# Reordering score tiles, reduction units, reciprocals and loads in the attention stage of a pooled-attention and two-MoE kernel

## The chip, the cores and the metric

The kernel runs on one core of a Trainium2 chip. The metric is device time in microseconds (us) of one execution. A core has five engines with instruction queues of their own: PE (TensorE, matmuls; its weight loads are listed as PEld), DVE (VectorE), ACT (ScalarE), POOL (GpSimd) and SP (SyncE, which here only issues transfers). Each queue runs strictly in its written order and waits on semaphores.

## The reference

```python
q_pool = q.reshape(B, H, S // factor, factor, D).mean(axis=3)       # B 4, H 8, S 1152, D 64, factor 2
scores = scale * np.matmul(q_pool, k.transpose(0, 1, 3, 2))
scores = scores - np.max(scores, axis=-1, keepdims=True)
attn = np.exp(scores)
attn = attn / (np.sum(attn, axis=-1, keepdims=True) + 1e-09)
x = np.matmul(attn, v)                    # then laid out as 2304 tokens x 512
h = x @ w_in;  x = (h - np.tanh(h)) @ w_out                         # 512 -> 2048 -> 512
h = x @ w_in2; x = (h * (1.0 / (1.0 + np.exp(-1.702 * h)))) @ w_out2
```

## The kernel before, in words

The attention stage comes first and takes about a third of the time; two MLP layers follow and are not touched here. The order of all instructions is written out by hand: what the code says first stands first in an engine's queue.

Attention works on 16 pairs of heads (`p`), each head on 64 of the 128 partitions, and each pair has two halves (`x` = 0 and 1, 288 pooled queries each). So there are 32 halves, `h = 2p + x`; "even" means x = 0. In a half, PE computes nine score tiles (S, `scores`, L429), each of four pairs of matmuls: keys' high part times queries' high part, keys' low part (`kl`), queries' low part (`ql`), and a selector matrix times `row`, which subtracts the row's maximum. ACT turns each tile into probabilities (`pf`, L435). Then PE multiplies them with v (`products`, L480) and sums them with ones (L493), and ACT copies the result out (`u`, L501).

The maxima for the next pair come from eleven units (`unit`): matmuls into an `mx` tile, which DVE reduces into a column of `mt` (L371). Units 0 to 8 of pair p+1 run within the halves of pair p; they are X (512 wide; unit 6 in four narrow pieces). Units 9 and 10 of a pair, called C, run in its own even half. The strings in `usual` say in which order tiles and units stand on PE: the first string for even halves, the second for odd ones. After unit 6 and after unit 10, `max_rows` and `send_rows` reduce `mt`, transpose it to `tt`, and send it by six (part 0) or four (part 1) small transfers on SP into `row` and `cr`. Part 0 is needed by the fourth step of the first score tile of the next pair's even half, part 1 by its odd half.

All tiles of PSUM (`sc`, `mx`, `acc`) come in rotation from four buffers, so a tile waits until the one four places earlier in PE's order has been read.

Sums of the probabilities are shared: POOL adds tiles into `sum` (L446), DVE adds the last four into `rest` (L464). The sums are gathered by four small transfers into `s9` (`sums`), `recip` takes the reciprocals on DVE (L522, L523) and writes them to `rd` in DRAM, `spread` reads `rd` back to all partitions (`rbd`, which waits for `rd` to land), and `normalise` multiplies (L540).

Jobs are hung on places of a half by `at(h, place, job)` and run in this order: "first", "start", tiles and units, "load", "pre", "gp", the products, "end", "pool". Loads of later pairs: keys `kr` (L290, 576 KB), `v` (576 KB) and pooled queries `qs` (288 KB) on SP; two transfers on POOL's queue add into DRAM (`qd`, L281 and L338). `prep_kl` on POOL waits for the last DVE job noted in `last["v"]`. MLP weights are prepared meanwhile: one weight takes four halves, one DVE step (L143, L149, L156 or L163) at "end" of each; the first step also takes magnitudes on ACT (`wa`, L142), at "end" of halves 2, 6, 10, ..., 26.

```python
at(h, "start", sums, p - 1)
at(h, "pre" if h == NH - 2 else "end", recip, p - 1)
at(h + 1, "start", spread, p - 1)
at(h + 1, "end", normalise, p - 1)
at(h - 4, "load", load_sum, p)
at(h - 4, "first", load_k, p)
```

Of the kernel before, what the change touches and what calls it, by code (L numbers as in the profile page):

```python
# [7 lines left out]
F32 = mybir.dt.float32  # L8
# [15 lines left out]
def f32(ap):  # L24
    return ap.bitcast(F32)
# [3 lines left out]
def tile_pooled_attention_two_moe(  # L29
# [11 lines left out]
    nc = tc.nc  # L41
# [87 lines left out]
    def after(job, first):  # L129
        if first is not None:  # L130
            tc.add_manual_dep(job.ins, first.ins.name, mybir.DependencyInfo(
                mybir.DependencyClass.Sync, mybir.DependencyReason.DATA), reason="port")

    def convert_steps(raw, hi, lo, shape, box, eng=None):
        def shift():
            box["t"] = wpool.tile([128, DM], I32, tag="wt", name="wt", bufs=2)
            if raw.dtype == F32:
                nc.scalar.activation(f32(box["t"][:]), raw, AF.Copy)
                return
            top = raw[:, :, 1]  # L140
            box["a"] = wpool.tile([128, DM], F32, tag="wa", name="wa", bufs=1)
            nc.scalar.activation(box["a"], f32(top), AF.Abs)  # L142
            nc.vector.tensor_scalar(  # L143
                out=box["t"], in0=top, scalar1=3, scalar2=0x3FFFFFF8,
                op0=ALU.logical_shift_left, op1=ALU.bitwise_and,
            )

        def sign():
            nc.vector.scalar_tensor_tensor(  # L149
                out=box["t"], in0=raw[:, :, 1], scalar=-0x40000000, in1=box["t"],  # L150
                op0=ALU.bitwise_and, op1=ALU.bitwise_or,
            )

        def flush():
            t, a = box["t"], box["a"]
            nc.vector.scalar_tensor_tensor(  # L156
                out=f32(t[:]), in0=a, scalar=2.0 ** -15 * 1.125, in1=f32(t[:]),
                op0=ALU.is_ge, op1=ALU.mult,
            )

        def tail():
            t = box["t"]
            nc.vector.scalar_tensor_tensor(  # L163
                out=t, in0=raw[:, :, 0], scalar=29, in1=t,
                op0=ALU.logical_shift_right, op1=ALU.bitwise_or,
            )

        def split():
            t = f32(box["t"][:]).rearrange("p (a b) -> p a b", a=shape)
            nc.scalar.activation(hi, t, AF.Copy)  # L170
            job = (eng or nc.gpsimd).tensor_tensor(lo, t, f32(hi), op=ALU.subtract)  # L171
            if eng is None:
                after(job, last.pop("rest", None))

        def nothing():
            pass

        bits = [sign, flush, tail] if raw.dtype == I32 else [nothing] * 3
        return [shift, *bits, split]

# [2 lines left out]
    def weight(kind, n):  # L183
        return slots[kind][n % NSLOT[kind]]

    def piece(kind, n):

        li, f = divmod(n, NQ * 4)
        if kind == "i":
            src = layers[li][0][f].rearrange("p (c f) -> p c f", c=NKC)  # L190
            shape = NKC
        else:
            src = layers[li][1][f * 128:(f + 1) * 128, :].rearrange("p (a d) -> p a d", a=1)
            shape = 1
        box = {}

        def ld():
            box["raw"] = load_piece(src, shape)

        def cv(j):  # L200
            def go():
                if "s" not in box:
                    w = weight(kind, n)
                    hi, lo = ((w[:, :, 0, :], w[:, :, 1, :]) if kind == "i"
                              else (w[:, 0:1, :], w[:, 1:2, :]))
                    late = nc.vector if kind == "o" and (n in (2, 3) or n >= NQ * 4 + 2) else None
                    box["s"] = convert_steps(box["raw"], hi, lo, shape, box, late)
                box["s"][j]()
            return go

        return [ld] + [cv(j) for j in range(5)]

    def joined(jobs, parts=((0,), (1, 2), (3, 4), (5,))):
        def together(js):
# [4 lines left out]
    def attention(ctx: ExitStack):  # L219
# [326 lines left out]
        def at(h, when, fn, *args):  # L546
            jobs.setdefault((h, when), []).append(lambda: fn(*args))

        def do(h, when):
            for job in jobs.pop((h, when), ()):  # L550
                job()

        usual = "S C S C S S X S S S X S S X X", "S X S S S X S R S S S X S X"
        begin = "S X S S S X S C S S S C S X X", "S X S S S X S S X S X S S R X X"
        NH = 2 * NPAIR
        todo, ahead = {}, {}
# [17 lines left out]
        order = (("i", 0), ("i", 1), ("o", 0), ("i", 2), ("i", 3), ("o", 1), ("o", 2), ("o", 3))  # L574
        slots_at = [h for h in range(2, NH - 1) for _ in range(1 if h < NH - 2 else 4)]
        for n, (kind, f) in enumerate(order):
            ld, shift, *more, split = piece(kind, f)
            mine = slots_at[4 * n:4 * n + 4]
            at(mine[0] - 1, "load", ld)
            at(mine[0], "pre" if mine[0] % 2 else "end", shift)  # L580
            for h, job in zip(mine[1:], more, strict=True):
                at(*((h, "end") if h < NH - 2 else (NH - 1, "pre")), job)
            at(mine[-1] + 1, "pre" if mine[-1] + 1 < NH - 1 else "end", split)
# [4 lines left out]
        for p in range(NPAIR):  # L588
            h = 2 * p
            if p > 0:  # L590
                at(h - 2, "load", load_v, p)
                if p == 1:
                    at(h - 2, "pre", prep_corner, p)
                    at(h - 2, "end", prep_ql, p)
                    at(h - 2, "pool", prep_kl, p, 0)
                    at(h - 1, "end", prep_kl, p, 1, nc.vector)
                else:
                    at(h - 2, "pool", prep_kl, p, 0)
                    at(h - 1, "pool", prep_kl, p, 1)
                    at(h - 1, "first", fetch_low, p, "ql")  # L600
                at(h, "start", sums, p - 1)
                at(h, "pre" if h == NH - 2 else "end", recip, p - 1)
                at(h + 1, "start", spread, p - 1)
                at(h + 1, "end", normalise, p - 1)
            if p > 1:
                at(h - 4, "start", new_pair, p)
                at(max(h - 6, 0), "start", load_one, p)
                at(max(h - 6, 0), "gp" if p > 2 else "start", load_other, p)
                at(h - 4, "load", load_sum, p)
                at(h - 4, "first", load_k, p)  # L610
                at(h - 3, "pre", prep_qh, p)
                at(h - 3, "pre", prep_corner, p)
                at(h - 3, "pre", minus_qh, p)
                at(h - 3, "pre", prep_kh, p, 0)
                at(h - 3, "pre", prep_kh, p, 1)
                at(h - 3, "gp", take_qh, p)
# [51 lines left out]
        for h in range(NH):  # L668
# [6 lines left out]
            for u in todo[h]:  # L675
# [11 lines left out]
                if u == (p + 1, 6):  # L687
                    max_rows(p + 1, 0)
                    send_rows(p + 1, 0)
                if u == (p, 10):  # L690
                    max_rows(p, 1)
                    send_rows(p, 1)
                if t == KT and late:
                    add_rest(p, x, late.pop(0))
                    if late and x == 0 and full(p, x):
                        add_rest(p, x, late.pop(0))
                        end_rows(p)
            while late:
                add_rest(p, x, late.pop(0))
            if h == NH - 2:  # L700
# [661 lines left out]
```

## Time and profile before

| what | value |
|---|---|
| median of 3 runs | 1172.92 us (1171.52 to 1174.12) |
| the profiled execution's own time | 1176.05 us |
| its span, first to last instruction | 1174.3 us |
| PE busy over the span | 1161.6 us (99%) |
| DVE / ACT / POOL busy | 992.5 (85%) / 652.9 (56%) / 453.6 us (39%) |
| mean granted TensorE clock | 0.998 |

Busy time counts from an instruction's start to its modelled end, so PE's 99% does not mean that it runs at its peak: a matmul that starts late behind a wait shows as the distance between starts, not as idle time. The attention stage lies at 0 to 392 us. Halves are found by the first L429 row with `sc<-qh,kh` after the L493 rows.

### The profile page before, as it was taken

The numbers are of one execution on the slowest core, as the hardware profiler recorded it, in microseconds if no ns is written. First come the engines' busy times: TensorE is split into PE (matmuls) and PEld (weight loads), VectorE is DVE, ScalarE is ACT, GpSimd is POOL, SyncE is SP. The second block draws the span as 40 slices with busy tenths as digits, with TensorE's granted clock in tenths as the row PEclk, the third lists the DMA queues.
The fourth block names the chain that finished last, engine by engine and source line by source line (L and its number), as shares of the span: only waits on it lengthen the run. The fifth ranks groups of instructions, "written<-read, shape, count | busy, mean of one in ns | idle before, by whom it ended". The sixth has DMA issues, their size and how long they took to land.

```text
span 1174.3 us, 23203 instructions
## 1 busy us (share of the span) xinstructions
PE 1161.6 (99%) x9260; PEld 971.5 (83%) x9260; DVE 992.5 (85%) x1242; ACT 652.9 (56%) x969; POOL 453.6 (39%) x321
## 2 busy tenths in 40 slices
PE   9999999999999999999999999999999999999998
PEld 7767676767777888888898898898889999999996
DVE  6888988878988799999999999998986899886442
ACT  4667566656665678676666666655654333342220
POOL 7667676766766223333232333221000222222211
PEclk9999999999999999999999999999999999999999
DMA  6455655555542021111111111112998757765512
GB/s 191 123 118 137 162 127 133 146 143 130 125 111 62 12 64 36 55 54 37 54 36 54 37 36 36 37 54 95 389 389 311 275 215 287 269 225 206 206 54 90
DMA packets 58221, 156.29 MB, mean 133 GB/s; under 512 B 14080, under 2 KB 19712, under 8 KB 58112
## 3 DMA queue, kind: packets, MB, share of 16 engines
q1 hardware_dynamic: 53536, 146.14, 35.8%
q0 software_dynamic: 4032, 8.26, 4.9%
q8 instruction: 73, 1.20, 0.4%
q10 hardware_dynamic: 544, 0.39, 0.1%
q14 instruction: 36, 0.29, 0.1%
HBM read 124.39 MB, written 33.69 MB: 135 GB/s over the span
## 4 chain that ended last, share of the span: by engine, by line
PE 77%; DVE 14%; ACT 4%; issue 2%; DMA 1%; POOL 1%; SPq 1%; DVEq 0%; ACTq 0%; POOLq 0%
PE sc L429 13%; PE y L1048 13%; PE y L1236 12%; PE h L1139 11%; PE acc L480 11%; PE b L996 5%; PE a L996 3%; PE c L996 3%; PE mx L359 3%; DVE work L1182 2%; DVE work L1199 2%; DVE wt L149 2%; DVE wt L143 1%; ACT work L1180 1%; PE acc L493 1%
## 5 line engine op out<-in xcount | busy, mean ns | idle before, releaser
L371 DVE TENSOR_REDUCE mt<-mx 128x2 fp32r<-128x1024 f32 (+2 forms) x176 | 198.1, 1136 | 41.0 <-PE mx L359 22.1
L435 ACT ACTIVATE pf<-sc 128x576 f32<-128x576 f32 x288 | 173.8, 655 | 24.2 <-PE sc L429 15.1
L1236 PE MATMUL y<-mem,big 128*128 128x512 f32 (+1 forms) x780 | 185.1, 368 | 1.2 <-POOL mem L1153 1.2
L1236 PEld LDWEIGHTS y<-mem,big 128*128 128x128 f32 x780 | 142.6, 188 | 21.2 <-POOL mem L1153 2.3
L1034 POOL TENSOR_TENSOR mem<-work,mem 128x768 fp32r<-128x768 f32 x24 | 46.2, 1938 | 289.4 <-ACT mem L1029 274.4
L446 POOL TENSOR_TENSOR sum<-sum,pf 128x576 f32<-128x576 f32 x95 | 137.4, 1446 | 29.2 <-DVE rest L464 23.9
L480 PE MATMUL acc<-pf,v 128*32 128x288 f32 x2304 | 146.3, 407 | 0.0
L1139 PE MATMUL h<-mem,big 128*128 128x512 f32 (+1 forms) x564 | 127.1, 377 | 0.0
L480 PEld LDWEIGHTS acc<-pf,v 128*32 128x32 f32 x2304 | 71.6, 110 | 65.6 <-ACT pf L435 5.0
L1139 PEld LDWEIGHTS h<-mem,big 128*128 128x128 f32 x564 | 104.4, 188 | 17.0
L1153 POOL TENSOR_TENSOR mem<-work,mem 128x1024 fp32r<-128x1024 f32 (+1 forms) x40 | 89.1, 2227 | 75.9 <-ACT mem L1151 75.9
L1048 PE MATMUL y<-big,mem 128*128 128x512 f32 x405 | 114.0, 390 | 0.0
L1201 ACT ACTIVATE work<-work 128x1024 f32<-128x1024 f32 (+1 forms) x40 | 39.1, 977 | 107.5 <-DVE work L1199 107.5
L429 PE MATMUL sc<-qh,kh 64*128 64x288 f32 x576 | 94.0, 315 | 0.0
L171 POOL TENSOR_TENSOR big<-wt,big 128x512 fp32r<-128x512 f32 x25 | 32.6, 1302 | 155.5 <-ACT big L170 142.5
L429 PE MATMUL sc<-row,sel 64*128 64x288 f32 x576 | 88.5, 293 | 3.9 <-DMA row<-tt 2.4
L1048 PEld LDWEIGHTS y<-big,mem 128*128 128x128 f32 x405 | 76.0, 188 | 15.5
L429 PE MATMUL sc<-qh,kl 64*128 64x288 f32 x576 | 87.5, 293 | 0.0
L429 PE MATMUL sc<-ql,kh 64*128 64x288 f32 x576 | 87.2, 292 | 0.0
L1139 PE MATMUL h<-mem,w 128*128 128x512 f32 (+1 forms) x376 | 84.7, 377 | 0.0
L501 ACT ACTIVATE u<-acc 128x576 f32<-128x576 f32 x30 | 19.6, 653 | 107.3 <-PE acc L493 107.3
L1139 PEld LDWEIGHTS h<-mem,w 128*128 128x128 f32 x376 | 69.6, 188 | 11.3
(176 smaller groups left out, 2580.5 us busy)
## 6 DMA issues: line engine op xcount, KB each, us to landing
mem<-x SPq DMA_DIRECT2D x36, 768.0 KB
big<-x SPq DMA_DIRECT2D x27, 768.0 KB
raw<-in_moe_w_in_dram SPq DMA_DIRECT2D x32, 512.0 KB
raw<-in_moe_w_out_dram SPq DMA_DIRECT2D x32, 512.0 KB
v<-in_v_dram SPq DMA_DIRECT2D x16, 576.0 KB
x<-big SPq DMA_DIRECT2D x12, 768.0 KB
kr<-in_k_dram SPq DMA_DIRECT2D x15, 576.0 KB
rbd<-rd SPq DMA_DIRECT2D x32, 144.0 KB
```

What stands on the lines that cost most here:

```text
L371: nc.vector.tensor_reduce(out, src, AX.X, ALU.max, negate=True)
L429: nc.tensor.matmul(sc[:, s, 0:HB], w[r], m[r, xs], start=(n == 0), stop=(n == 3))
L435: nc.scalar.activation(pf, sc[:, :, 0:HB], AF.Exp, scale=SCALE)
L446: job = nc.gpsimd.tensor_add(out, parts[p, x], new)
L480: nc.tensor.matmul(acc[32 * n:32 * n + 32, 0], pairs[p]["v"][:, s, t, 32 * h:32 * h + 32], new[t][:, s, :], start=(t == 0), stop=(t == KT ...
L996: nc.tensor.matmul(bank[nm][:, fp, 0:G], w[:, wo, a, 128 * c:128 * c + 128], x[:, b, c, :], start=(k == 0), stop=(k == 5))
L1034: eng.tensor_tensor(g[:, :, 1], halves[n][:, fp], f32(g[:, :, 0]), op=ALU.subtract)
L1048: nc.tensor.matmul(y, gts[2 * side + fp][:, j, r, 128 * t:128 * t + 128], wo[:, p, :], start=(k == 0), stop=(k == len(terms) - 1))
L1139: nc.tensor.matmul(hb[:, j, 0:TBS[b]], wi[:, c, w, :], x[r][c], start=(k == 0), stop=(k == 3 * NKC - 1))
L1153: eng.tensor_tensor(gt[:, :, 1, :], g, f32(gt[:, :, 0, :]), op=ALU.subtract)
L1201: nc.scalar.activation(a, u, AF.Relu, bias=-T2)
L1236: nc.tensor.matmul(ys[m][:, 0:w], lhsT, rhs, start=(fp == 0 and not low and j == p == 0), stop=(fp == 1 and low and j == 1))
```

## The change

Five edits, all in the attention stage:

- In the even halves from 2 to 28, the first unit X stands after the third score tile instead of the fourth, and the second after the sixth instead of the seventh; the last two still stand at the end.
- In these halves the part-1 maxima (`max_rows(p, 1)`, `send_rows(p, 1)`) stand on DVE after unit 0 of the next pair instead of after unit 10.
- `recip` moves from "end" of the even half to a new place "rows", straight after DVE's last `rest` adds and `end_rows` and ahead of the half's loads; its transfer `rd` moves on SP with it, ahead of `v` and `qs`. `load_k` moves from "first" to "load", behind `v` and `qs`.
- The weight steps note themselves in `last["v"]`, so `prep_kl` on POOL waits for the half's weight step where that is the last DVE job ahead of it.
- The magnitudes `wa` are taken at "pre", ahead of the products, instead of at "end".

```diff
+    def size(raw, box):
+        if raw.dtype != F32:
+            box["a"] = wpool.tile([128, DM], F32, tag="wa", name="wa", bufs=1)
+            nc.scalar.activation(box["a"], f32(raw[:, :, 1]), AF.Abs)
...
-            box["a"] = wpool.tile([128, DM], F32, tag="wa", name="wa", bufs=1)
-            nc.scalar.activation(box["a"], f32(top), AF.Abs)
-            nc.vector.tensor_scalar(
+            if "a" not in box:
+                size(raw, box)
+            last["v"] = nc.vector.tensor_scalar(
...
-        usual = "S C S C S S X S S S X S S X X", "S X S S S X S R S S S X S X"
+        usual = "S C S C S X S S S X S S S X X", "S X S S S X S R S S S X S X"
...
+            at(mine[0], "pre", first)
...
-                at(h, "pre" if h == NH - 2 else "end", recip, p - 1)
+                at(h, "pre" if h == NH - 2 else "rows", recip, p - 1)
...
-                at(h - 4, "first", load_k, p)
+                at(h - 4, "load", load_k, p)
...
-                if u == (p, 10):
+                if u == ((p + 1, 0) if 1 < h < NH - 2 and x == 0 else (p, 10)):
                     max_rows(p, 1)
                     send_rows(p, 1)
...
                         end_rows(p)
+                        do(h, "rows")
```

The other three weight steps get `last["v"] =` in the same way. The changed file's line numbers are five or six higher.

PE's queue in half 8, from its second C unit to its first X unit (`sc` are the steps of score tiles, `mx` the units). Before:

```order
L366 MATMUL mx<-kh,cq_95 128x288 x4
L429 MATMUL sc<-qh,kh 128x288 x2
L429 MATMUL sc<-qh,kl 128x288 x2
L429 MATMUL sc<-ql,kh 128x288 x2
L429 MATMUL sc<-row_97,sel 128x288 x2
L429 MATMUL sc<-qh,kh 128x288 x2
L429 MATMUL sc<-qh,kl 128x288 x2
L429 MATMUL sc<-ql,kh 128x288 x2
L429 MATMUL sc<-row_97,sel 128x288 x2
L359 MATMUL mx<-kh,qh 128x512 x2
```

And of the change:

```order
L372 MATMUL mx<-kh,cq_95 128x288 x4
L435 MATMUL sc<-qh,kh 128x288 x2
L435 MATMUL sc<-qh,kl 128x288 x2
L435 MATMUL sc<-ql,kh 128x288 x2
L435 MATMUL sc<-row_97,sel 128x288 x2
L365 MATMUL mx<-kh,qh 128x512 x2
L435 MATMUL sc<-qh,kh 128x288 x2
L435 MATMUL sc<-qh,kl 128x288 x2
L435 MATMUL sc<-ql,kh 128x288 x2
L435 MATMUL sc<-row_97,sel 128x288 x2
```

The unit has moved ahead of the fourth tile's four steps.

DVE's queue in the same half, from the reductions of the C units (`mt_86`, `x2`) to the first of the next half (`r` are the reciprocals). Before:

```order
L371 TENSOR_REDUCE mt_86<-mx 128x2 x2
L378 TENSOR_REDUCE m_88<-mt_86 128x4
L383 STREAM_TRANSPOSE tt<-m_88 128x32
L371 TENSOR_REDUCE mt_90<-mx 128x2 x2
L464 TENSOR_TENSOR rest<-pf 128x576
L371 TENSOR_REDUCE mt_90<-mx 128x2
L464 TENSOR_TENSOR rest<-rest,pf 128x576 x2
L394 TENSOR_REDUCE row_96<-cr_98 128x64
L371 TENSOR_REDUCE mt_90<-mx 128x2
L156 SCALAR_TENSOR_TENSOR wt<-wa,wt 128x512
L522 TENSOR_REDUCE r_2135<-s_101 128x9
L523 RECIPROCAL r_2135<-r_2135 128x9
```

And of the change, from the first X unit's reduction on:

```order
L377 TENSOR_REDUCE mt_90<-mx 128x2
L384 TENSOR_REDUCE m_88<-mt_86 128x4
L389 STREAM_TRANSPOSE tt<-m_88 128x32
L377 TENSOR_REDUCE mt_90<-mx 128x2
L470 TENSOR_TENSOR rest<-pf 128x576
L377 TENSOR_REDUCE mt_90<-mx 128x2
L470 TENSOR_TENSOR rest<-rest,pf 128x576 x2
L400 TENSOR_REDUCE row_96<-cr_98 128x64
L528 TENSOR_REDUCE r_2080<-s_101 128x9
L529 RECIPROCAL r_2080<-r_2080 128x9
L377 TENSOR_REDUCE mt_90<-mx 128x2
L161 SCALAR_TENSOR_TENSOR wt<-wa,wt 128x512
```

The maxima now follow the first X unit's reduction, and the two reciprocal instructions stand ahead of the last unit's reduction and of the weight step.

SP's queue over an even and an odd half (`s` are the sums, `row` and `cr` the maxima). Before:

```order
L290 DMA kr<-in_k_dram 128x1152
L514 DMA s_101<-u 64x1x9 x4
L278 DMA qd<-in_q_dram 128x576
L388 DMA row_96<-tt 1x4x32 x2
L388 DMA cr_98<-tt 1x4x32 x2
L294 DMA v<-in_v_dram 128x1152
L285 DMA qs<-qd 128x576
L525 DMA rd<-r_2135 128x9
L342 DMA ql<-qd 128x576
L531 DMA rbd<-rd 64x576 x2
L388 DMA row_97<-tt 1x4x32 x6
```

And of the change:

```order
L520 DMA s_101<-u 64x1x9 x4
L284 DMA qd<-in_q_dram 128x576
L394 DMA row_96<-tt 1x4x32 x2
L394 DMA cr_98<-tt 1x4x32 x2
L531 DMA rd<-r_2080 128x9
L300 DMA v<-in_v_dram 128x1152
L291 DMA qs<-qd 128x576
L296 DMA kr<-in_k_dram 128x1152
L348 DMA ql<-qd 128x576
L537 DMA rbd<-rd 64x576 x2
L394 DMA row_97<-tt 1x4x32 x6
```

`rd` has moved ahead of `v` and `qs`, and `kr` from the head of the even half to the place between `qs` and `ql`. On ACT, `wa` stands ahead of the copy `u` instead of behind it; POOL's order is the same.

## Rows read from the trace of the kernel before

**Rows 1.** The page, busy time: engine, us, share of the span, instructions.

```profile
PE 1161.6 (99%) x9260; PEld 971.5 (83%) x9260; DVE 992.5 (85%) x1242; ACT 652.9 (56%) x969; POOL 453.6 (39%) x321
```

**Rows 2.** Timeline of PE (start, us, what): half starts; one wait, at 253.68.

```profile
86.44 0.40 PE L429 MATMUL sc<-qh,kh 64*128 64x288 f32 x2
...
99.65 0.41 PE L429 MATMUL sc<-qh,kh 64*128 64x288 f32 x2
...
111.26 0.40 PE L429 MATMUL sc<-qh,kh 64*128 64x288 f32 x2
...
122.95 0.40 PE L429 MATMUL sc<-qh,kh 64*128 64x288 f32 x2
...
134.43 0.40 PE L429 MATMUL sc<-qh,kh 64*128 64x288 f32 x2
...
180.90 0.40 PE L429 MATMUL sc<-qh,kh 64*128 64x288 f32 x2
...
193.33 0.40 PE L429 MATMUL sc<-qh,kh 64*128 64x288 f32 x2
...
251.43 0.40 PE L429 MATMUL sc<-qh,kh 64*128 64x288 f32 x2
...
253.68 0.57 PE L429 MATMUL sc<-row,sel 64*128 64x288 f32 x2 [1.59 <-DMA row<-tt]
...
266.68 0.40 PE L429 MATMUL sc<-qh,kh 64*128 64x288 f32 x2
```

**Rows 3.** Windows: stretch, busy PE PEld DVE ACT POOL, granted clock, DMA share, GB/s.

```profile
121.00:123.00 2.00, 2.00 (x38) 0.86 (x30) 1.91 (x3) 0.00 (x0) 0.13 (x1) 1.00 0.93 353
254.00:257.60 3.60, 3.60 (x33) 3.60 (x34) 1.90 (x4) 1.74 (x3) 1.02 (x1) 0.53 0.56 166
```

**Rows 4.** Waits of SP's queue, 40 to 380 us: total us, times, longest.

```profile
SPq L531 <- DMA rd<-r: 32.4, 14, 4.6
```

**Rows 5.** Timeline of SP, `rbd` and `row` of half 5, `row` of half 9.

```profile
80.76 1.15 SPq L531 DMA_DIRECT2D rbd<-rd  x2
82.00 3.28 SPq L388 DMA_DIRECT2D row<-tt  x6
...
128.68 3.29 SPq L388 DMA_DIRECT2D row<-tt  x6
```

**Rows 6.** Transfers by queue, 85.5 to 88 us: packets, MB, share of 16 engines.

```profile
q0 software_dynamic: 137, 0.28, 88.6%
```

**Rows 7.** Timeline of PE, end of half 8 and second unit of half 9.

```profile
117.11 0.92 PE L359 MATMUL mx<-kh,qh 64*128 64x512 f32 x4
117.96 4.57 PE L480 MATMUL acc<-pf,v 128*32 128x288 f32 x72
...
125.41 0.39 PE L359 MATMUL mx<-kh,qh 64*128 64x512 f32 x2
```

**Rows 8.** Timeline of DVE, halves 8 and 9.

```profile
116.26 1.23 DVE L371 TENSOR_REDUCE mt<-mx 128x2 fp32r<-128x1024 f32 x1 [0.59 <-PE mx L359]
117.40 1.41 DVE L464 TENSOR_TENSOR rest<-pf 128x576 f32<-128x576 f32 x1
...
121.96 1.21 DVE L371 TENSOR_REDUCE mt<-mx 128x2 fp32r<-128x1024 f32 x1
...
123.69 0.18 DVE L522 TENSOR_REDUCE r<-s 128x9 f32<-128x27 f32 x1
...
124.03 1.22 DVE L371 TENSOR_REDUCE mt<-mx 128x2 fp32r<-128x1024 f32 x1
```

**Rows 9.** Timeline of POOL, half 8.

```profile
115.25 2.94 POOL L446 TENSOR_TENSOR sum<-sum,pf 128x576 f32<-128x576 f32 x2
```

**Rows 10.** Timeline of ACT, halves 7, 8 and 9.

```profile
100.34 0.66 ACT L142 ACTIVATE wa<-raw 128x512 f32<-128x512 f32 x1
...
112.95 5.03 ACT L435 ACTIVATE pf<-sc 128x576 f32<-128x576 f32 x8 [0.17 <-PE sc L429]
...
134.56 0.65 ACT L501 ACTIVATE u<-acc 128x576 f32<-128x576 f32 x1 [2.01 <-PE acc L493]
```

More of the change, by code (lines that the diff above doesn't have):

```diff
@@ L148, in sign @@
         def sign():
-            nc.vector.scalar_tensor_tensor(
+            last["v"] = nc.vector.scalar_tensor_tensor(
                 out=box["t"], in0=raw[:, :, 1], scalar=-0x40000000, in1=box["t"],
@@ L155, in flush @@
             t, a = box["t"], box["a"]
-            nc.vector.scalar_tensor_tensor(
+            last["v"] = nc.vector.scalar_tensor_tensor(
                 out=f32(t[:]), in0=a, scalar=2.0 ** -15 * 1.125, in1=f32(t[:]),
@@ L162, in tail @@
             t = box["t"]
-            nc.vector.scalar_tensor_tensor(
+            last["v"] = nc.vector.scalar_tensor_tensor(
                 out=t, in0=raw[:, :, 0], scalar=29, in1=t,
@@ L184, in weight, with piece @@
         return slots[kind][n % NSLOT[kind]]
-    def piece(kind, n):
+    def piece(kind, n, ahead=False):
         li, f = divmod(n, NQ * 4)
@@ L209, in cv @@
             return go
-        return [ld] + [cv(j) for j in range(5)]
+        first = [lambda: size(box["raw"], box)] if ahead else []
+        return [ld, *first, *(cv(j) for j in range(5))]
     def joined(jobs, parts=((0,), (1, 2), (3, 4), (5,))):
@@ L576, in attention @@
         for n, (kind, f) in enumerate(order):
-            ld, shift, *more, split = piece(kind, f)
+            ld, first, shift, *more, split = piece(kind, f, True)
             mine = slots_at[4 * n:4 * n + 4]
             at(mine[0] - 1, "load", ld)
+            at(mine[0], "pre", first)
             at(mine[0], "pre" if mine[0] % 2 else "end", shift)
```

## The prediction, made before the change was run

> **What bounds the kernel now.** I read the page first: PE is busy 99% of the span [rows 1], so nothing off PE counts unless PE starts something later because of it. For a PE that never looks idle the distance between starts is the view to read, so I took the timeline of PE next and measured the halves of the attention stage from first score row to first score row [rows 2]. An undisturbed even half, half 8, takes 122.95 - 111.26 = 11.69 us; odd half 9 takes 11.48 and odd half 7 takes 11.61. Three even halves stand out: half 6 with 13.21, half 14 with 12.43 and half 20 with 15.25. Against 11.69 they lose 1.52, 0.74 and 3.56, together 5.8 us. In half 20 the row at 253.68 says why: the fourth step of the first tile waited 1.59 us for the transfer into `row`. The granted clock of the next 3.6 us was 0.53 on average [rows 3], that is mostly the lower of the two levels, 1.2 GHz, after an engine that had stood still; that is part of the 3.56.
>
> Why is `row` late? The waits of SP's queue [rows 4] show `rbd` waiting 32.4 us in 14 times, up to 4.6, for `rd` to land, and the six `row` transfers stand behind `rbd`. In half 5 `rbd` goes out at 80.76 and the six issue from 82.00 to 85.28, which is 1.16 us before half 6 starts; in half 9 they issue from 128.68 to 131.97, 2.46 before half 10 [rows 2, 5]. From 0.94 us before half 6 an accumulating transfer of POOL's queue takes 88.6% of all engines for 2.5 us [rows 6], and what has not landed by then waits behind it. So the point that decides is an issue that ends some 1.2 us or less before the next half.
>
> The median of the runs is 1172.92, and the profiled execution took 1176.05, 3.1 more. My sum stands against 1176.05; without the three waits it would have taken 1170.2, a little under the fastest run (1171.5), so the runs shown probably hold some such waits each, and on average some 2.7 us.
>
> **Reciprocals and `kr`.** The reciprocals now end on DVE ahead of the last unit's reduction. DVE's work up to there keeps its place (next part but one), so they end at 121.96 + 0.34 = 122.30, the 0.34 being the two instructions from 123.69 to 124.03 [rows 8]; before, they ended at 124.03. That is 1.7 us, and above all `rd` no longer stands behind 576 KB of `v` and 288 KB of `qs`. It leaves at about +11.1 of the even half and has until SP has issued `v`, `qs`, `kr` and `ql`. So `rbd` follows at once, and `row` is issued as soon as `tt` is there, as in half 9.
>
> What is moved with it counts too. `v` and `qs` leave 2.5 us later, and `kr` joins them: `v`, `qs`, `kr`, `ql` and `rbd` make 2016 KB (2.06 MB) in one row. At 353 GB/s, measured while `v` and `qs` ran [rows 3], that is 5.8 us; one accumulating transfer falls into it, 2.5 us x 88.6% = 2.2 us [rows 6]. From about +12.6 (one microsecond after the issue of `v`, an estimate) this ends at +20.6, which is +9.1 of the odd half. The last `row` issue ends at 131.97 - 122.95 = +9.0, its packets about 1 us later, +10.0; the next accumulation starts at about +10.5. So the rows still come first, with half a microsecond to spare. `kr` has landed after `v`, `qs` and itself, 1.47 MB or 4.2 us, and the 2.2: at +19.0, which is +7.5 of the odd half. ACT copies it last before `u` and is done with that at 134.56 - 2.01 = 132.55, +9.6 [rows 10]; the 2.01 idle behind it means that a delay up to that costs nothing. Term: -5.8 us, bounds 0 (every wait comes back) and -5.8.
>
> The Trainium skill speaks against this edit ("DMA: Bandwidth & Descriptors", section "Queues, rings and completion order"): each transfer engine takes the descriptors of one ring in their order, so six small transfers cannot pass the 576 KB of keys now put in front of them. No row here shows the order within a ring; by the rule the result is the slower rival below, by the rows the bulk ends first.
>
> **Units three tiles apart.** At the end of half 8 the last two units start at 117.11 and the products at 117.96 [rows 7]: 0.85 for two units. The last unit takes over the buffer of the second unit, whose reduction ran from 116.26 to 117.49 after DVE had idled 0.59 waiting for PE [rows 8]. With the second unit one tile (some 0.53 us) earlier, that reduction ends near 116.96 and the third unit, which now takes that buffer, finds it free at 117.11. The next limit is ACT: the products take the buffer of the eighth tile. The eight exponentials of tiles 2 to 9 run without a gap, 5.03 us [rows 10], 0.63 each, so the eighth tile's ends at 117.35. In the new order the fourth tile comes 0.23 later, which lets ACT idle once for up to 0.26, and the eighth ends by 117.63. The products can start at about 117.7 to 117.8. I take 0.2 us of 117.96 - 117.70 = 0.26 in each of 14 even halves (2 to 28): -2.8 us. Bounds: 0 (ACT is the limit altogether) and -0.26 x 14 = -3.6.
>
> DVE does not follow. Its first `rest` addition starts at 117.40 and takes 1.41 us, to 118.81; POOL's sums run until 115.25 + 2.94 = 118.19 [rows 8, 9], and I read it as held until then and running for the 0.62 behind. Started sooner it would still end when it does now, so the last unit's reduction would start where the reciprocals end, 122.30 instead of 121.96, and the next half's first reduction at 124.03 as before. The second unit of half 9 needs that reduction's end, 125.25; it starts at 125.41 today [rows 7] and would want to start at 125.21. It waits 0.04 plus up to 0.1 for a weight load that can't run ahead; I take 0.12 in the seven pairs whose even half has a weight step as long as half 8's, and nothing in the seven with the shorter first step: +0.8. Bounds: 0 and 14 x 0.2 = 2.8, the whole gain.
>
> **Magnitudes.** In seven odd halves (3, 7, ... 27) `wa` stands ahead of the first exponential for 0.66 us [rows 10]; PE pays 11.61 - 11.48 = 0.13 [rows 2]. Ahead of the products ACT only waits, so: -0.9 us, bounds 0 and -0.9.
>
> **Part-1 maxima and `kl`.** The maxima move one reduction later on DVE, but SP is no longer blocked by `kr` at the half's head, so they leave no later: 0. `kl` in the even halves waits for the weight step, which ends about when the reciprocals ended (124.03): 0. If `kl` ran across DVE's step instead, the price would be that of the `rest` addition above, 1.41 - 0.62 = 0.8 us of DVE.
>
> **Sum:** 1176.05 - 5.8 - 2.8 + 0.8 - 0.9 = **1167.4 us**, 5.5 (0.47%) under the median of the runs. About 0.2%, 2.3 us, is what a measurement of this kernel tells from no change.
>
> **The rivals.** *The rows stay late at times.* For it: `rd` is one transfer among large ones, half a microsecond of room is little, and the accumulating transfers remain. Against it: `rd` now goes ahead of all of them. Then the runs keep their waits and get only the rest: 1172.92 - 2.8 + 0.8 - 0.9 = 1170.0.
>
> *DVE gives the units' gain back.* For it: DVE follows its neighbours without a gap from 117.40 to 125.25. Then 1176.05 - 5.8 - 0.9 = 1169.4.
>
> *The rows fall behind the keys* (slower). If the bulk runs 1.4 us longer than I work out, it ends past +10.5 and the accumulation goes ahead of the rows in every odd half; each such half then costs what half 6 lost, 1.52. In 13 even halves (4 to 28) that is 19.8; in half of them 9.9, so 1167.4 + 9.9 = 1177.3. For it: 576 KB more directly ahead. Against it: 353 GB/s was measured with small gaps, not at its best.
>
> **How the numbers follow.** The forecast gets 0.50, with a range of its own of 1164.2 to 1169; rows late at times 0.25; gain given back 0.15; rows behind keys 0.10. Below 1170.6 (faster by over 0.2%) lie the forecast, nearly all of the third and about half of the second: 0.75. Same: the other half of the second and a rest: 0.15. Slower: 0.10. The range: down to 1164.2, which is the median of the runs less the full 8.7 of the sum, if the profiled execution is only long by a fixed amount; up to 1171.3, which takes in the second rival with a wait more.
>
> **What would show it.** No even half over 12 us from 4 to 28, no 0.5 level of the clock; `rbd` waiting under 1 us; the six `row` issues ending 2 us or more ahead of each next half. The two last units of an even half in 0.65 instead of 0.85. Odd halves alike at 11.5 to 11.6. I am wrong if `row` waits appear in most halves, if ACT waits for `kr`, or if the pairs stay at 23.2 us.

## The result and the profile after

The changed kernel took 1180.07 us (median of 6 runs, 1178.12 to 1184.15) beside 1172.22 for the kernel before (6 runs, 1170.2 to 1175.01): a ratio of 1.0067, with a 95% interval of 1.0045 to 1.0089. It is slower by 0.7%, where 1167.4 was forecast. The profiled execution took 1180.33 us, 4.28 more than that of before.

The page of the changed kernel, span and busy time:

```profile
span 1178.6 us, 23215 instructions
PE 1161.5 (99%) x9260; PEld 971.7 (82%) x9260; DVE 996.0 (85%) x1242; ACT 655.1 (56%) x969; POOL 452.8 (38%) x321
```

Beside [rows 1] nothing tells the two apart: PE is busy for the same time, since a matmul that starts late is no idle time. The distance between the starts of halves does tell. The timeline of PE of the changed kernel, first rows of halves 6 to 11, the rows that wait in halves 6 and 8, the end of half 8 and the second unit of half 9:

```profile
87.56 0.40 PE L435 MATMUL sc<-qh,kh 64*128 64x288 f32 x2
88.49 0.36 PE L435 MATMUL sc<-row,sel 64*128 64x288 f32 x1 [0.27 <-issue]
89.76 0.37 PE L435 MATMUL sc<-row,sel 64*128 64x288 f32 x1 [0.90 <-DMA row<-tt]
...
100.77 0.40 PE L435 MATMUL sc<-qh,kh 64*128 64x288 f32 x2
...
112.31 0.40 PE L435 MATMUL sc<-qh,kh 64*128 64x288 f32 x2
114.42 0.37 PE L435 MATMUL sc<-row,sel 64*128 64x288 f32 x1 [1.32 <-issue]
...
119.87 0.64 PE L365 MATMUL mx<-kh,qh 64*128 64x512 f32 x4
120.43 4.57 PE L486 MATMUL acc<-pf,v 128*32 128x288 f32 x72
125.42 0.40 PE L435 MATMUL sc<-qh,kh 64*128 64x288 f32 x2
...
127.97 0.50 PE L365 MATMUL mx<-kh,qh 64*128 64x512 f32 x2
...
137.10 0.40 PE L435 MATMUL sc<-qh,kh 64*128 64x288 f32 x2
...
148.53 0.40 PE L435 MATMUL sc<-qh,kh 64*128 64x288 f32 x2
```

Half 10 shows what an undisturbed even half now takes, 11.43 us instead of 11.69 [rows 2]. Halves 6 and 8 take 13.21 and 13.11, and what starts late in each is the subtraction of the maxima, as at 253.68 of before (in half 6 both of its matmuls, with waits of 0.27 and 0.90). Odd half 9 takes 11.68 (11.48 before), half 7 11.54 (11.61 before). Measured in this way, seven even halves lose to `row`: 4, 6, 8, 12, 16, 20 and 22, by 0.95, 1.77, 1.68, 1.73, 1.42, 1.40 and 3.57 over 11.43, together 12.5 us. Before it was 5.8 in three.

So the profiled executions add up: waits +6.7, fourteen even halves at -0.26 (-3.6), seven odd halves like half 9 at +0.19 (+1.3), six like half 7 at -0.07 (-0.4), and half 3, which is 0.15 longer than before: +4.2 of the 4.28.

Why is `row` late again? The waits of SP's queue of the changed kernel, 40 to 380 us (total us, times, longest):

```profile
SPq L531 <- DVE r L529: 62.7, 14, 5.0
...
SPq L394 <- DMA kr<-in_k_dram: 10.0, 11, 2.1
SPq L394 <- DMA ql<-qd: 6.4, 12, 1.7
SPq L537 <- DMA rd<-r: 5.3, 7, 1.3
```

The wait of [rows 4] has gone as forecast: `rbd` waits 5.3 us for `rd` instead of 32.4. In its place the `row` issues themselves (L394) wait 16.4 us, for `kr` and for `ql` to land. The timeline of SP of the changed kernel in half 7, beside [rows 5]:

```profile
100.47 0.33 SPq L531 DMA_DIRECT2D rd<-r  x1
100.90 0.37 SPq L300 DMA_DIRECT2D v<-in_v_dram  x1
101.36 0.38 SPq L291 DMA_DIRECT2D qs<-qd  x1
101.84 0.38 SPq L296 DMA_DIRECT2D kr<-in_k_dram  x1
102.31 0.38 SPq L348 DMA_DIRECT2D ql<-qd  x1
102.79 1.32 SPq L537 DMA_DIRECT2D rbd<-rd  x2
106.56 5.33 SPq L394 DMA_DIRECT2D row<-tt  x6
```

Count back eight issues from the fifth `row`: it is `kr`. From the sixth: `ql`. No data connects them with `row`; SP waits at an issue until the transfer that it issued eight places earlier has landed. The trace's semaphores say why it is eight: the program has the landing of SP's transfers told on eight semaphores in turn (534 of 535 issues carry that of the issue eight places earlier), and an issue waits until the transfer last told on its semaphore has landed. `kr` landed at 109.22, and the fifth `row` was issued at 109.23; `ql` landed at 111.38, and the sixth was issued at 111.40. The `row` transfers of the changed kernel at 105 to 116 us (their number, ns of one issue, first and last start):

```profile
L394 SPq DMA_DIRECT2D row<-tt x6: 492/492/550, 106.6 to 111.4; - x6
```

The six take 5.33 us instead of the 3.28 of [rows 5] and end at 111.89, 0.42 ahead of half 8. The windows of the changed kernel over the same stretch (columns as in [rows 3]) show what that meets:

```profile
103.00:110.30 7.30, 7.30 (x114) 5.52 (x114) 6.44 (x9) 6.72 (x13) 6.37 (x6) 1.00 0.96 311
110.30:111.50 1.20, 1.20 (x28) 0.64 (x21) 1.09 (x2) 0.20 (x1) 0.68 (x1) 1.00 0.10 28
111.50:113.00 1.50, 1.50 (x23) 0.82 (x15) 1.45 (x4) 0.55 (x1) 0.00 (x0) 1.00 1.07 131
```

The large transfers end at about 110.3, +9.5 of the half, but for some last packets that follow one another until 111.55. So the engines are nearly idle for 1.2 us, in which the rows would have had room, but the last of them is only issued from 111.40 to 111.89. From 111.5 the accumulating transfer of POOL takes everything, and this row waits behind it: the packets of the first five rows move at 109.90 to 110.64, those of the sixth at 113.35 to 113.80.

The other halves agree. Ahead of the seven even halves that lose, the sixth row is issued at +9.98 to +10.81 of the odd half; ahead of the six that don't (10, 14, 18, 24, 26 and 28), at +8.72 to +9.60.

### The profile page after: what moved, and what is told of

Its sections match the earlier page's. It is cut to its first block, busy times and chain, and to the rows that moved or that the text cites. A ratio compares the mean times of both kernels' runs of the same rounds, so it can differ in the third digit from the quotient of the medians.

```text
span 1178.6 us, 23215 instructions
## 1 busy us (share of the span) xinstructions
PE 1161.5 (99%) x9260; PEld 971.7 (82%) x9260; DVE 996.0 (85%) x1242; ACT 655.1 (56%) x969; POOL 452.8 (38%) x321
## 4 chain that ended last, share of the span: by engine, by line
PE 49%; DVE 11%; ACT 3%; issue 2%; POOL 1%; DVEq 0%; ACTq 0%; POOLq 0%
PE y L1244 13%; PE y L1056 12%; PE h L1147 12%; PE b L1004 5%; PE a L1004 3%; PE c L1004 3%; DVE work L1207 2%; DVE work L1190 2%; DVE wt L148 1%; DVE wt L154 1%; ACT work L1188 1%; DVE wt L161 1%; DVE xb L1264 1%; ACT mem L106 1%; DVE wt L168 1%
## 5 line engine op out<-in xcount | busy, mean ns | idle before, releaser
L1032 ACT ACTIVATE work<-work 128x768 f32<-128x768 f32 x36 | 29.5, 844 | 86.5 <-DVE work L1027 82.8
```

## The experiments

Each edit is made to the changed kernel ("after") or to the kernel before. "Waits" are the even halves from 4 to 28 that lose over 0.15 us to a wait in the profiled execution. The ratio is to the kernel before on the same chip, whose medians were 1174.37 (first four rows), 1173.78 (next four) and 1173.50 (last four).

| kernel | us | ratio (95%) | waits | even; odd like 9; odd like 7 |
|---|---|---|---|---|
| k_first | 1167.87 | 0.9941 (0.9924 to 0.9957) | none | 11.45; 11.67; 11.55 |
| k_behind_rbd | 1171.40 | 0.9980 (0.9966 to 0.9994) | 8, 12, 16, 22, 24 | 11.44; 11.67; 11.55 |
| k_only | 1171.23 | 0.9974 (0.9962 to 0.9987) | 8, 20, 26 | 11.70; 11.48; 11.60 |
| units_only | 1171.33 | 0.9978 (0.9963 to 0.9993) | 8, 20 | 11.45; 11.67; 11.60 |
| rd_behind_loads | 1167.93 | 0.9957 (0.9943 to 0.9972) | none | 11.44; 11.67; 11.55 |
| recip_only | 1181.16 | 1.0070 (1.0054 to 1.0087) | none | 11.70; 11.80; 13.1 |
| k_behind_sums | 1167.63 | 0.9955 (0.9940 to 0.9969) | none | 11.44; 11.67; 11.54 |
| k_behind_sums_recip_at_load | 1168.09 | 0.9958 (0.9943 to 0.9973) | 12 | 11.44; 11.66; 11.49 |
| recip_and_kl | 1170.35 | 0.9971 (0.9960 to 0.9982) | none | 11.70; 11.47; 11.61 |
| k_behind_sums_no_kl_wait | 1191.42 | 1.0153 (1.0132 to 1.0173) | none | 11.44; 12.04; 16.15 |
| rd_behind_loads_recip_at_load | 1167.84 | 0.9952 (0.9934 to 0.9970) | none | 11.44; 11.67; 11.50 |
| wa_only | 1174.13 | 1.0004 (0.9989 to 1.0020) | 8, 22 | 11.70; 11.48; 11.48 |

Four theories were weighed. **Landing** (L): the rows are late because SP, eight issues on, waits for the keys to land. **Bytes** (B): they are late because the keys' 576 KB stand directly ahead of them. **Held** (H): landing is late only because `rd`, put ahead of the loads, holds SP until DVE's reciprocals are done, so that all loads leave in the odd half. **Guard** (G): `kl`'s new wait for the weight step is what keeps POOL off DVE, and so carries the earlier reciprocals. The expectations name three more: **R**, that `rd`, waiting for DVE, makes everything behind it on SP late by itself; **K**, that the keys behind `v` and `qs` cost wherever `rd` stands; **D**, that the early reciprocals on DVE cost.

### Where the keys stand: k_first, k_behind_rbd, k_only, k_behind_sums

k_first is "after" with the keys back at the head of the even half.

```diff
-                at(h - 4, "load", load_k, p)
+                at(h - 4, "first", load_k, p)
```

> Edit: the changed kernel with one part undone: the key load stands at the head of the even half again. Theory L (a transfer on SP waits until the transfer eight issues before it has landed; with the keys and ql issued eight places ahead of the fifth and sixth row transfers, these wait for them): SP's waits of rows on kr and ql, 16.4 us in 23 times in the changed kernel, go to under 2; the row waits of PE at the head of halves 4, 6, 8, 12, 16, 20 and 22 (12.5 us) mostly go; 1166 to 1170 us. Theory B (the row packets lie behind the keys' bytes in the rings, no matter how SP waits): the bytes are gone from there too, so the same time. Theory R (rd, waiting for DVE ahead of v and qs, blocks SP and makes everything behind it late): rd stays where it is, so the row waits stay, above 1176 us.

It took 1167.87 us, and the waits have gone. The timeline of SP of k_first in half 7, where eight issues ahead of the last two rows stand `qs` and `ql`:

```profile
97.65 0.37 SPq L300 DMA_DIRECT2D v<-in_v_dram  x1
98.12 0.38 SPq L291 DMA_DIRECT2D qs<-qd  x1
98.59 0.38 SPq L348 DMA_DIRECT2D ql<-qd  x1
99.07 1.26 SPq L537 DMA_DIRECT2D rbd<-rd  x2
103.32 3.28 SPq L394 DMA_DIRECT2D row<-tt  x6
```

The rows need 3.28 us again and end at 106.60, 2.48 ahead of half 8 at 109.08. `v` leaves as late in its half as in the changed kernel (97.65 - 97.52 = +0.1), so the place of the keys decides here, and R alone is out. Whether by landing or by bytes, the next kernel tells.

k_behind_rbd puts the keys between `rbd` and the rows, directly ahead of them.

```diff
-                at(h - 4, "load", load_k, p)
+                at(h - 3, "start", load_k, p)
```

> Edit: the changed kernel with the key load issued in the odd half, between rbd and the six row transfers, so it is under eight issues ahead of all six rows but its 576 KB lie directly ahead of their bytes. Theory L: no row waits for kr on SP, the row issues end 2 us ahead of the next half, 1167 to 1172 us; a later kr costs nothing on ACT up to 2 us. Theory B: the row packets come 1.6 us (576 KB at 353 GB/s) later than in the half without keys there and fall behind the accumulation in most halves, 1176 us or more. Theory R: unchanged, about 1180.

It took 1171.40: less bad than the changed kernel, with the keys' bytes nearer to the rows. That speaks against B as the cause, and the waits of SP's queue of k_behind_rbd, 40 to 380 us, count as L does:

```profile
SPq L394 <- DMA ql<-qd: 2.6, 5, 1.0
SPq L520 <- DMA kr<-in_k_dram: 2.6, 5, 0.7
SPq L394 <- DMA rbd<-rd: 1.7, 7, 0.5
```

With `kr` two issues further back, the fifth row's partner is `ql`, the sixth's the first `rbd`, and `kr`'s partner is a transfer of the sums (L520): each name in the list is the one eight places ahead. In half 9 of this kernel the rows leave from 127.37 without a gap, 1.35 us behind the keys, and half 10 has no wait. Half 8 shows another cost. The waits of k_behind_rbd at 108 to 113 us:

```profile
ACT kh L327 <- DMA kr<-in_k_dram: 3.1, 1, 3.1
...
PE mx L372 <- ACT u L507: 0.4, 1, 0.4
```

The keys land so late that ACT waits 3.1 us for them, 1.1 more than the 2.01 it has to spare [rows 10]; the half is 12.32 long, 0.88 more. Halves 12 and 24 do wait for `row`, 0.97 and 0.93 us. Ahead of both the sixth row is held until +9.8; ahead of half 24 the packets of the first rows move only from +10.4 on, behind the keys, so there the bytes have a share too.

k_only makes this edit alone, on the kernel before: the keys go behind `v` and `qs`, and `rd` stays behind all three.

```diff
-                at(h - 4, "first", load_k, p)
+                at(h - 4, "load", load_k, p)
```

> Edit: the kernel before with nothing but the key load moved from the head of the even half to behind v and qs. Theory L: kr leaves at about +9.2 of the even half, 2 to 3 us earlier than in the changed kernel, and has landed before the row that is eight issues behind it, so rows do not wait for it on SP; but rd now stands behind 576 KB more, rbd waits about 1.6 us longer for it, and rows are as late as in half 5 of the kernel before in most halves: 1176 to 1184 us. Theory B: rows come after the keys' bytes in any case, 1176 us or more. Theory R: the reciprocals stand where they stood, so no loss: 1171 to 1174.

L and B both missed: it is faster, 1171.23, in R's range, though R was out by k_first. Here `rd` stands behind the loads, and they leave at +5.9 to +8.2 of the even half, `v` five microseconds earlier than in the changed kernel (and some two earlier than before, where `kr` at the half's head holds SP: 43.7 us of waiting for `kl`, in 12 times); they have landed long before the rows. So the keys' place is harmful only together with something else. That led to H.

k_behind_sums takes "after" and puts the keys behind the four sums at the even half's start, ahead of `rd`:

```diff
-                at(h - 4, "load", load_k, p)
+                at(h - 4, "start", load_k, p)
```

> Edit: the changed kernel with the key load directly behind the four sums of the even half instead of behind v and qs. It does not hold the sums back (its place at the head does, until kl has been taken) and is not held back by rd. Theories H and K: no row waits, sums and part-1 maxima leave 1 to 2 us sooner than with the keys at the head, which nothing waits for; 1166 to 1169 us, the same as with the keys at the head within 0.2%. Theory D: above 1174.

1167.63 and no wait: like k_first.

### Where `rd` stands: rd_behind_loads

"After", with the reciprocals early on DVE as they are and the keys behind `v` and `qs` as they are; only the transfer `rd` goes back behind the loads on SP.

```diff
             last["v"] = nc.vector.reciprocal(r9, r9)
-            rd = drpool.tile([128, QJ], F32, tag="rd", name="rd", bufs=2)
-            nc.sync.dma_start(out=rd, in_=r9)
-            norm[p]["rd"] = rd
+            norm[p]["r9"] = r9
...
+                    at(h, "end", send_rd, p - 1)
```

> Edit: the changed kernel, in which only the transfer rd moves back behind the loads on SP; the reciprocals stay early on DVE, the keys stay behind v and qs. Theory H (rd in front of the loads holds v, qs and kr back until DVE has taken the reciprocals, at about +11 of the even half, so kr and ql land late and the fifth and sixth row transfers, eight issues behind them, wait): the loads leave at about +6.3 to +7.3, as in the kernel with only the keys moved, no row waits for kr or ql, no even half from 4 to 28 over 12 us; 1165 to 1169 us. Theory K (the keys behind v and qs are what costs, wherever rd stands): still above 1174 us. Theory D (the early reciprocals on DVE cost): above 1174 us too.

1167.93, no wait: H, and neither K nor D. The timeline of SP of rd_behind_loads in half 8:

```profile
117.06 0.39 SPq L300 DMA_DIRECT2D v<-in_v_dram  x1
117.55 0.37 SPq L291 DMA_DIRECT2D qs<-qd  x1
118.02 0.38 SPq L296 DMA_DIRECT2D kr<-in_k_dram  x1
121.02 0.32 SPq L536 DMA_DIRECT2D rd<-r  x1
```

The half starts at 109.88, so the keys leave at +8.1 instead of beyond its end, and `rd` at +11.1. In this kernel `rbd` waits 38.5 us for `rd`, 15 times, more than the 32.4 of [rows 4], and no row is late: it is not the length of that wait that counts but when it ends. The latest `rbd` leaves at +5.0 of its half here (half 21), and at +5.8 and +6.4 in halves 5 and 19 of the kernel before, the two ahead of its longest halves.

### One part alone: units_only, wa_only, recip_only, recip_and_kl

units_only is the kernel before with the new strings and the maxima's new place.

```diff
-        usual = "S C S C S S X S S S X S S X X", "S X S S S X S R S S S X S X"
+        usual = "S C S C S X S S S X S S S X X", "S X S S S X S R S S S X S X"
...
-                if u == (p, 10):
+                if u == ((p + 1, 0) if 1 < h < NH - 2 and x == 0 else (p, 10)):
```

> Edit: the kernel before with nothing but the unit order of the even halves and the place of the part-1 maxima changed. All theories: the two last units of an even half in 0.57 instead of 0.85 us, 14 times -0.26 = -3.6; odd halves behind a long weight step +0.1 to +0.2, seven times; row waits as before (5.8 us in the profile of before). 1168 to 1172 us; if DVE gives all back, 1171 to 1174.

Even halves go from 11.69 to 11.45, those like half 9 from 11.48 to 11.67, and those like half 7 stay: 14 x -0.24 + 7 x 0.19 = -2.0 us; the ratio gives -2.6, and the row waits stay as well.

wa_only is the kernel before with the magnitudes ahead of the products.

```diff
+            at(mine[0], "pre", first)
```

> Edit: the kernel before with nothing but the magnitudes taken ahead of the products. Odd halves 7, 11, ... 27 go from 11.60 to 11.48, seven times -0.12, 0.8 us in all, less than the time of one run to the next tells: 1171 to 1174 us, to be read in the profile's halves. If ACT's place for them is not free, even halves 2, 6, ... get longer than 11.69.

Odd halves like 7 fall by the expected 0.12, to 11.48. In the runs' time that does not show (1.0004), being less than the rows' waits vary.

recip_only is the kernel before with the reciprocals and `rd` at the new place, and nothing else.

```diff
-                at(h, "pre" if h == NH - 2 else "end", recip, p - 1)
+                at(h, "pre" if h == NH - 2 else "rows", recip, p - 1)
...
+                        do(h, "rows")
```

> Edit: the kernel before with nothing but the reciprocals and rd moved ahead of the loads; the keys stay at the head of the even half. Theory H: v and qs leave late, but nothing that rows wait for is late, and rbd goes out at once, so the row waits go: 1166 to 1170 us. Theory K: the same. Theory D: slower than before, above 1174 us.

1181.16, slower by 0.7%, and without a single row wait. Only D had it slower, and D was out by rd_behind_loads, which has the early reciprocals and is fast. Halves 7, 11, 15, 19 and 23 take 13.1 (half 27 takes 12.3). The timelines of DVE, then POOL, then PE of recip_only in half 7:

```profile
98.67 1.16 DVE L371 TENSOR_REDUCE mt<-mx 128x2 fp32r<-128x1024 f32 x1
99.75 2.42 DVE L143 TENSOR_SCALAR wt<-raw 128x512 int32<-128x512 int32 x1
102.10 1.21 DVE L371 TENSOR_REDUCE mt<-mx 128x2 fp32r<-128x1024 f32 x1
```

```profile
99.58 0.85 POOL L281 DMA_DIRECT2D qd<-in_q_dram  x1
100.16 1.73 POOL L328 TENSOR_TENSOR kl<-kr,kh 128x576 fp32r<-128x576 f32 x1
```

```profile
103.37 0.50 PE L359 MATMUL mx<-kh,qh 64*128 64x512 f32 x2 [1.28 <-DVE mt L371]
```

The weight step (0.45 before) takes 2.42 us: it starts while POOL prepares a transfer, and ends at 102.17, 0.28 behind POOL's `kl`. PE's unit waits for the reduction behind it. In the kernel before, `kl` waited for the reciprocals, which stood behind the weight step; moved ahead, they let `kl` go. It is the wait added in `last["v"]` that prevents this in the changed kernel. recip_and_kl adds it:

```diff
-            nc.vector.tensor_scalar(
+            last["v"] = nc.vector.tensor_scalar(
```

> Edit: the kernel before with the reciprocals and rd ahead of the loads (as in the run that took 1181) and kl behind the weight steps; nothing else. Theory G (with the reciprocals early, kl is no longer held until DVE's weight step is done; the first step, a single-tensor operation, then waits for POOL's kl and takes 2.4 instead of 0.42 us, and PE waits for the reduction behind it): the step is back at 0.42 to 0.46, the fifth step of odd halves 7, 11, 15, 19, 23, 27 is back at 0.53 from 2.08, and with the row waits gone the time is 1167 to 1171 us. If it stays above 1176, the early reciprocals themselves cost.

1170.35, all halves as in the kernel before, and no row wait: G. The ratio, 0.9971, is what the row waits cost an average run of the kernel before: some 3.4 us of 1173.5.

k_behind_sums_no_kl_wait is the converse: the fast k_behind_sums without that wait.

```diff
-            last["v"] = nc.vector.tensor_scalar(
+            nc.vector.tensor_scalar(
```

> Edit: the changed kernel with the keys behind the sums (1167.6) and kl's wait for the weight steps taken out again. Theory G: the first weight step waits for kl in up to seven halves, 2 us on DVE each, of which PE loses about 1.5; 8 to 13 us more, 1175 to 1181 us. If kl's wait is worth nothing, 1167 to 1169.

1191.42; the sign was expected, the size not. Halves 7, 11, 19 and 23 take 16.1 to 16.2 us. The timelines of DVE and POOL of k_behind_sums_no_kl_wait in half 7:

```profile
99.10 3.77 DVE L148 TENSOR_SCALAR wt<-raw 128x512 int32<-128x512 int32 x1
```

```profile
98.92 0.85 POOL L287 DMA_DIRECT2D qd<-in_q_dram  x1
99.50 1.72 POOL L334 TENSOR_TENSOR kl<-kr,kh 128x576 fp32r<-128x576 f32 x1
100.93 1.64 POOL L452 TENSOR_TENSOR sum<-pf 128x576 f32<-128x576 f32 x1
```

Here the step does not get in between `kl` and the next sum either, and ends 0.30 behind the sum. PE's unit waits 2.96 us for the reduction behind it, and in the 3.6 us from 104.60 the granted clock is 0.53, mostly the lower level: so the half loses 4.6 us where the step takes 3.3 more. The odd halves like 9 take 12.04, since the long step ahead of them takes 1.05 to 1.06 us instead of 0.68. In the changed kernel itself, with the wait, the seven steps take 416 to 419 ns (their source line, 40 to 380 us):

```profile
L148 DVE TENSOR_SCALAR wt<-raw x7: 416/418/419, 52.6 to 341.6; 128x512 int32<-128x512 int32 x7
```

### Reciprocals behind the last unit: two variants

Both put the reciprocals behind the last unit's reduction on DVE; the first is otherwise k_behind_sums, the second rd_behind_loads.

```diff
-                at(h, "pre" if h == NH - 2 else "rows", recip, p - 1)
+                at(h, "pre" if h == NH - 2 else "load", recip, p - 1)
```

> Edit: as the one before, and the reciprocals one reduction later on DVE: behind the even half's last unit and ahead of the weight step. The last unit's reduction then ends 0.34 us sooner, so the second score tile of the odd half no longer waits for its buffer; the reduction behind it stands where it stood. Odd halves 0.05 to 0.1 us shorter, 14 times: 1 us less than the one before, 1165 to 1168. If the odd halves are held by the reduction behind the weight step alone, no difference.

> Edit: the changed kernel with rd behind the loads on SP and the reciprocals behind the last unit on DVE. Theory H: all loads leave at about +6.3, no row waits; odd halves 3, 7, ... 0.05 us shorter than with early reciprocals; 1166 to 1168 us.

1168.09 and 1167.84. The odd halves like 7 win 0.05 us more each and half 3 wins 0.15, 0.4 in all, which the runs cannot tell from nothing. All the versions from 1167.6 to 1168.1 are alike within their intervals, 0.4 to 0.6% faster than the kernel before; k_first needs the least: one word of the change undone.

## Why the prediction was wrong

**The step that failed** is the one under *Reciprocals and `kr`*: "The last `row` issue ends at 131.97 - 122.95 = +9.0, its packets about 1 us later", and with it "So the rows still come first, with half a microsecond to spare". The +9.0 came from half 9 of before, in which the last two rows stand eight issues behind `rd` and `ql`; it was kept for a queue in which they stand behind `kr` and `ql`. The bulk of the large transfers did end about when the working said (+9.1; about +9.5 in half 7), and the accumulation began about when it said (+10.5; 111.5 - 100.77 = +10.7). But the rows, which were to be behind nobody, waited at their issue for exactly those transfers to land, and the last was issued by +11.1. That landing was later than the bulk's end, too: `ql` landed at +10.6. The term of -5.8 became +6.7.

Two readings were off without deciding it. Half 14 of before lost its 0.74 with the `row` issues ending 1.47 us ahead of it (176.07 + 3.36, the half at 180.90), so the "1.2 us or less" was drawn too narrow. And `v` leaves some 3.3 us later, not 2.5 (+11.6 against +8.1 to +9.0 in most halves).

What makes the landing so late is the edit itself. The earlier `rd` was counted as a gain ("`rd` no longer stands behind 576 KB"), and its other side was seen and not priced: "`v` and `qs` leave 2.5 us later, and `kr` joins them". k_only and rd_behind_loads show that the keys behind `v` and `qs` are harmless while `rd` stands behind them, k_first and k_behind_sums that the early `rd` is harmless while the keys are issued ahead of it. With the rest of the change in place, either one alone gives 1167.6 to 1167.9; both give 1180.07.

**The rival that came** is nearest to *The rows fall behind the keys*: 1177.3 with a chance of 0.10. Its outcome was right: the accumulation goes ahead of a row in half of the even halves, for 12.5 us where it had 9.9. Its condition, that the bulk ends past +10.5, was nearly met: the last packets ended at +10.1 to +11.0 ahead of the seven halves. Its mechanism, that the rows come late because the keys' bytes are ahead of them, was not what decided. The Trainium skill ("DMA: Bandwidth & Descriptors", section "Queues, rings and completion order"), quoted there against the edit, has each engine take the descriptors of one ring in their order. The trace of the changed kernel agrees: the first five rows, issued from 106.56 to 109.72, move their packets at 109.90 to 110.64, when the bulk is through. But these five had landed by 111.95, ahead of the 112.81 at which PE comes to the step; the sixth was not in the ring yet. And k_behind_rbd puts the keys closer to the rows and loses less.

**What was right.** The other terms, seen without the row waits in k_first, whose profiled execution took 1167.64 us where the sum said 1167.4. That it comes so close is in part luck: the units gave some 0.6 us more than forecast, DVE took 0.5 more back, the magnitudes gave 0.7 less, and these errors partly cancel.

- Row waits of before: without them "it would have taken 1170.2". recip_and_kl, which has none and differs in nothing else that costs, took 1170.29 in its profiled execution. That early reciprocals cure the waits, by letting `rbd` go earlier, was right too.
- Units: 0.2 forecast for each even half, 0.25 measured, near the bound of 0.26. The two last units start 0.56 ahead of the products (119.87, 120.43) instead of 0.85 [rows 7].
- What DVE gives back: 0.12 in seven odd halves forecast, 0.19 measured. The timeline of DVE of the changed kernel, halves 8 and 9:

```profile
119.70 1.82 DVE L470 TENSOR_TENSOR rest<-pf 128x576 f32<-128x576 f32 x1
...
125.02 1.16 DVE L377 TENSOR_REDUCE mt<-mx 128x2 fp32r<-128x1024 f32 x1
126.70 1.22 DVE L377 TENSOR_REDUCE mt<-mx 128x2 fp32r<-128x1024 f32 x1
```

  The first `rest` addition is longer than in [rows 8], 1.82 instead of 1.41, as read there: started sooner, it ends with POOL's sums all the same. The half's first reduction ends at 127.92, and the second unit starts at 127.97, 2.55 into the half instead of 2.46.
- Magnitudes: 0.13 forecast, 0.12 measured alone, 0.06 together with the rest, where the reciprocals ahead of the last reduction take 0.05 of it back (the two variants above).
- `kl` at 0 was right, because of the added wait. The price named for its absence, 0.8 us of DVE, was too low: 2.0 in recip_only (2.42 - 0.45) and 3.3 in k_behind_sums_no_kl_wait.
- `kr` late for ACT: 4.1 us of waits in five halves, up to 1.6, inside the 2.01 allowed. k_behind_rbd shows the other side of that bound.

Of the signs named, "`row` waits appear in most halves" came, in 7 of 13; "ACT waits for `kr`" came in five halves, at no cost; "the pairs stay at 23.2" did not: undisturbed pairs take 23.0 and 23.1.

Left open: why `ql` lands by +9.6 in some halves and only after +9.9 in others of one execution (four of the seven are those in which an accumulating transfer issued at +0.5 shares the time of the bulk), and whether fewer, larger row transfers, which would shift the count of eight, would do as well as k_first; that wasn't tried. Nor was a kernel with more than eight of these semaphores.

## What to carry to other kernels

Before moving a transfer on a queue, write the queue's issues in a row and look not only at what stands directly ahead but at what stands as many places ahead of each urgent transfer as the program has semaphores for the queue's landings (eight here), since its issue may wait for that one to land; a queue that holds a small early transfer for an engine also holds every load behind it. Where two moves each look free, work out the place of the second with the first already made: here the kernel with either alone is 0.4 to 0.6% faster than before, and with both 0.7% slower. An instruction moved forward also gives up what others were made to wait for behind it, as `kl` did when the reciprocals went ahead of the weight step.

## What the runs showed that was not expected

- SP's issues wait for the landing of the transfer eight issues earlier, also where no data connects the two, since the program's eight semaphores come in turn: 16.4 us in 23 times in the changed kernel, and in k_behind_rbd for `ql`, `rbd` and, at the sums, `kr`, as the count names them.
- A DVE instruction with one tensor as input, 0.42 us long alone, took 2.42 us beside POOL's `kl` and 3.77 us beside `kl` and the sum behind it. The Trainium skill ("SBUF — State Buffer", section "SBUF: two separate sides") says that DVE, in a 2-port mode or with two inputs in SBUF, and GpSimd share a pair of ports by a lock: whichever starts first holds it for its whole instruction, and the other is blocked. That the step waits agrees, though no trace here names its mode. But in both runs it had started ahead of `kl`, at 99.75 and 99.10, and let `kl` pass, in the second run the sum too; that section does not say so.
- After the longest row wait PE ran at the lower clock, as in [rows 3]. The row that waits in half 22 of the changed kernel, then the window from 282.00 on, with the last 0.4 us of the wait in it:

```profile
282.37 0.37 PE L435 MATMUL sc<-row,sel 64*128 64x288 f32 x1 [1.69 <-DMA row<-tt]
```

```profile
282.00:286.00 4.00, 3.63 (x32) 3.66 (x34) 1.66 (x3) 1.87 (x3) 1.15 (x1) 0.61 0.44 144
```

  The granted clock of 0.61 is mostly the lower level, 1.2 GHz, after an engine that had stood still for 1.69 us. That half lost 3.57 us. Halves 6 and 8, with waits of 1.17 (in two parts) and 1.32, kept a granted clock of 1.00 in the 3.6 us behind them and lost 1.77 and 1.68.
